# A backward pass over a KV cache: the third boundary and the opening of the last pass put into written order

## The chip, the cores and the metric

The kernel runs on one core of a Trainium2 chip. The metric is device time in microseconds, lowest wins. Three runs of the kernel before gave 1979.25 to 1979.58 us, median 1979.43. One further execution was profiled; it took 1976.74 us, and the views of the profile (the page, windows, waits, timeline) come from it.

The engines: PE is TensorE (PEld its weight loads), DVE is VectorE, ACT is ScalarE, POOL is GpSimd, SP is SyncE, which here only issues transfers. SPq, ACTq and POOLq are the queues on which these engines issue DMA.

## What is computed

Two attention layers and two MLP layers alternate (A, B, A, B, with the same weights both times), for one token; the kernel returns the output and the gradients of all weights and of the KV cache.

```python
def _A_ref(x, k_cache, v_cache, wq, wo):          # 32 heads of 128, 4 KV groups, 65536 positions
    q = (x @ wq).reshape(B, Sq, Hq, Dh).transpose(0, 2, 1, 3)
    k = jnp.repeat(k_cache, rep, axis=1)
    v = jnp.repeat(v_cache, rep, axis=1)
    p = _softmax(jnp.einsum("bhqd,bhkd->bhqk", q, k) * (Dh ** -0.5), axis=-1)
    o = jnp.einsum("bhqk,bhkd->bhqd", p, v)
    return o.transpose(0, 2, 1, 3).reshape(B, Sq, Hq * Dh) @ wo

def _B_ref(x, w1, b1, w2, b2):                    # D = 1024, F = 3584
    r = jnp.maximum(jnp.einsum("bsd,df->bsf", x, w1) + b1, 0)
    return jnp.einsum("bsf,fd->bsd", r * r, w2) + b2

x = x + _A_ref(_layernorm(x), K, V, wq, wo);  x = x + _B_ref(_layernorm(x), w1, b1, w2, b2)
x = x + _A_ref(_layernorm(x), K, V, wq, wo);  x = x + _B_ref(_layernorm(x), w1, b1, w2, b2)
out, vjp = jax.vjp(f, x, K, V, wq, wo, w1, b1, w2, b2);  grads = vjp(grad_out)
```

## The kernel before

K and V are 67 MB each and don't fit on the chip, so the kernel makes four passes over them: forward attention of the first layer, forward of the second, backward of the second (scores' gradients and the query's), and a last pass that does the first layer's backward and writes the gradients of K and V for both layers together. Between passes lie boundaries, in which the MLP and the layernorms run and few bytes of K and V are used. The third boundary is the one between pass three and the last pass.

**The boundary.** With `dn3` from pass three, a layernorm backward (`ln_bwd`) gives `dx2`. A product with the transposed W2 gives the hidden gradient `dh2` (L1418 to L1422). Then eight dot products per partition are needed, one for each of the eight 128-row blocks of W1 (3584 long) with `dh2`: the class `RowDots`. Its method `plan` (L530) takes a list of steps. "B" is a row done on DVE and ACT: DVE multiplies the row with a broadcast of `dh2`, ACT sums it, each in two halves of 1792. "A" does both in one DVE operation per half. "P" is done on PE: eight transposes of 128 columns into a PSUM buffer, a copy to SBUF, eight matmuls of one column; four such groups a row (the last of four). "T" is like "P" with the transposes made earlier and in place. The broadcast of `dh2` (`bcast_vec`) fills area 6. A second `ln_bwd` gives `dx1`, a product with eight transposed Wo blocks (`wo_turn`, `first_transposed`) gives `dOT`, and `finish` makes from it the delta of the softmax's backward.

**The last pass** (`attn_bwd4`, L1013) is a pipeline of items, each of 8 positions' columns by 128; 64 items are a group and 32 columns (four items) a block `b`. Step `i` runs `vT(i)` (transposes of V and their evacuation), `vS(i - 2)` (matmuls of V with `dOT`, four items to a PSUM buffer; the buffer begins with a matmul that writes minus delta, and when it is full DVE multiplies it with the exponentials of both layers, POOL copies these beside it, and PE transposes the result into X^T) and `k8(i - 7)`: the query's gradient (`dq`) and two PSUM buffers of K and V gradients, evacuated by ACT or DVE, whichever has less `load`. After four items the block's gradients go to HBM on POOL's queue, 1 MB for K and 1 MB for V. `bg` holds work to be done at given steps.

**What sets the order.** The framework puts the instructions in an order of its own, within their dependencies; `in_order` (L607) ties the first instruction of a piece, on each engine, to the one before it. SP issues the transfers in written order and stands at one whose buffer isn't free. Buffers of 1 MB are `area[0..13]` and the four `e1_halves` (the exponentials of the first layer, which are parked in HBM and fetched back from `e1_away` at the end of the boundary). `ring.slot()` gives the buffer used longest ago, `ring.once` gives some areas for one time first. Areas 6 to 11 are, pair by pair, the stages of the pass's outputs. The lines around which the change lies:

```python
w1s: seven rows into ring slots (four of them e1_halves), the eighth into area[5]
for st, b in ((1, 0), (1, 2), (0, 0), (1, 3), (0, 1)):       # V 0, V 2, K 0, V 3, K 1
    streams[st].fetch(ORD4[0], b)
rd = RowDots(DC, F, dh2[:], "B2_dn", area[6], lambda: transpose(w1s[0]))
steps = [("B", 5), ("T", 0), ("P", 1), ("B", 4), ("P", 2), ("A", 7), ("B", 6), ("P", 3)]
ring.once(area[6]); streams[1].fetch(ORD4[0], 1)              # V 1, when area 6 has been read
for g in ORD4: nc.sync.dma_start(out=e_tiles[1][g], in_=e1_away[g][:, :])
og1.later(vbx1, ORD4[1], bg, 16, 5, first_rows, 30, nc.sync)  # 8 Wo rows, 256 KB each, on SP
```

`later` fetches Wo rows ahead of their dot products for the next group's `dOT`; `first_rows` has seven buffers, the first seven fetches come before the pass's own.

Of the kernel before, what the change touches and what calls it, by code (L numbers as in the profile page):

```python
# [14 lines left out]
P = 128  # L15
# [3 lines left out]
def kernel(  # L19
# [24 lines left out]
    nc = tc.nc  # L44
    NOSYNC = mybir.DependencyInfo(mybir.DependencyClass.NoSync, mybir.DependencyReason.DATA)
    D = A_x.shape[-1]
# [390 lines left out]
    class RowDots:  # L437
# [92 lines left out]
        def plan(self, steps, wt):  # L530


# [39 lines left out]

        def result(self):
            if self.pieces == 1:
                return self.y[:, :, 0]
            s = vec.tile([P, self.y.shape[1]], F32, name="rd_sum", tag="rd_sum", bufs=2)
            nc.vector.tensor_tensor(out=s[:], in0=self.y[:, :, 0], in1=self.y[:, :, 1], op=ALU.add)
            return s[:, :]
# [23 lines left out]
    def blocks(ap, i, n=1):  # L602

        return ap[:, i * 1024:(i + n) * 1024].rearrange("p (a b) -> p a b", b=P)


    def in_order(fn):  # L607

        insts = nc.cur_bb.bb.instructions
        n0 = len(insts)  # L610
        before = {}
        fn()
        new = list(insts[n0:])
        want = {i.engine for i in new}
        k = n0 - 1
        while want - set(before) and k >= max(0, n0 - 4000):
            before.setdefault(insts[k].engine, insts[k])
            k -= 1
        for i in new:
            p = before.pop(i.engine, None)  # L620
            if p is not None:
                tc.add_manual_dep(i, p.name, NOSYNC, reason="in_order")

    def pipeline(n, stages, bg=None):
        maxlag = max(l for _, l in stages)
        for i in range(n + maxlag):
            for fn, lag in stages:
                if 0 <= i - lag < n:
                    fn(i - lag)
            for fn in (bg or {}).pop(i, ()):  # L630
                in_order(fn)
        assert not bg, sorted(bg)
# [175 lines left out]
    class OutGrad:  # L808
# [28 lines left out]
        def first_transposed(self, g, dx, wT):  # L837
            dxb = tmp.tile([P, DC], BF, name="dx_b")
            nc.vector.tensor_copy(out=dxb[:], in_=dx[:])
            py = ps_bg([P, R], F32)  # L840
            for k in range(R):
                for i in range(DC):
                    nc.tensor.matmul(py[:, k:k + 1], lhsT=wT[k][i], rhs=dxb[:, i:i + 1], start=(k == 0 and i == 0),
                                     stop=(k == R - 1 and i == DC - 1), skip_group_check=True)
            nc.vector.tensor_copy(out=self.dOT[:, g * R:(g + 1) * R], in_=py[:, :])
            self.finish(g)
# [166 lines left out]
    def attn_bwd4(La, Lb, oga, ogb, order, eTa, eTb, dqT, bg, group_done, streams, more_stage, tail):  # L1013
# [3 lines left out]
        KT = Turn([blocks(small, i) for i in range(3)])  # L1017
# [7 lines left out]
        state = {}  # L1025
        kstream, vstream = streams

        def g_setup(g):
# [3 lines left out]
            nc.vector.tensor_copy(out=DOB[:, g, 0, R:R2], in_=ogb.dOT[:, sl])  # L1032
            CCf = tmp.tile([P, R4], F32, name="CCf")
# [14 lines left out]
            nc.vector.tensor_copy(out=ndt4[:, :, 0:R], in_=oga.nd2[:, sl].unsqueeze(1).to_broadcast([64, UB4, R]))  # L1048
            nc.vector.tensor_copy(out=ndt4[:, :, R:R2], in_=ogb.nd2[:, sl].unsqueeze(1).to_broadcast([64, UB4, R]))
            state[("G", g)] = GG  # L1050

# [10 lines left out]
        def vS(idx):  # L1062
            g, c8 = kit[idx]
            if idx == 0:
                g_setup(g)
            vt = state.pop(("vt", idx))
            for i in range(8):
                c = c8 + i
                slot = c % UB4
                if slot == 0:  # L1070
                    state["ps_dp"] = ps_sc([P, UB4, R2])
                    nc.tensor.matmul(state["ps_dp"][:, :, :].rearrange("p c r -> p (c r)"), lhsT=sel2[:, :],
                                     rhs=state[("ndt", g)][:, :, :].rearrange("o c r -> o (c r)"), start=True, stop=False)
# [4 lines left out]
                                 rhs=DOB[:, g, 0:w, :].rearrange("p a b -> p (a b)"), start=False, stop=last)  # L1078
                if last:
                    c0 = c - slot  # L1080
# [8 lines left out]
                    nblk = UB4 // 4  # L1089
                    pt2 = ps_tr()  # L1090
                    for bi in range(nblk):
                        nc.tensor.transpose(pt2[:, bi, :], X[:, 4 * bi:4 * bi + 4, :].rearrange("p a b -> p (a b)"), ident_b[:, :])
                    xt = XT.next()
                    evac(xt[:, 0:nblk, :], pt2[:, 0:nblk, :])
                    state[(g, c0 // UB4)] = (X, xt)
# [20 lines left out]
        def k8(idx):  # L1116
            g, c8 = kit[idx]
            if idx < n - 4:
                dq(idx)
            elif idx == n - 4:  # L1120
                for k in range(4):
                    dq(idx + k)
            u = c8 // UB4
# [24 lines left out]
            if idx >= n - 8:  # L1148
# [11 lines left out]
        pipeline(n, [(vT, 0), (vS, TLEAD), (k8, TLEAD + UB4 // 8 + 1)], bg)  # L1160
# [232 lines left out]
    wo_here = [view for _, view in slabs(A_wo, ORD4[0] * GD, R, 0, D)]  # L1393
    woT1 = {}

    def wo_turn(*ks):
        for k in ks:
            transpose(wo_here[k], None, k % 2 == 0)
            woT1[k] = [part(wo_here[k], i, P) for i in range(DC)]
    w1s = []  # L1400

    def fetch_w1b(a=None):
        v = (a if a is not None else ring.slot())[:, 0:F]
        nc.sync.dma_start(out=v, in_=B_w1[len(w1s) * P:(len(w1s) + 1) * P, :])
        w1s.append(v)
    for _ in range(7):
        fetch_w1b()
    qg3.wT = wqT
    dn3 = qg3.last_transposed(ORD3[-1])
    fetch_w1b(area[5])  # L1410
    in_order(lambda: wo_turn(0, 1))
# [4 lines left out]
    in_order(lambda: wo_turn(2, 3))  # L1416
# [7 lines left out]
    ring.remove(*e1_halves)  # L1424
    ring.once(*area[7:12])
    for st, b in ((1, 0), (1, 2), (0, 0), (1, 3), (0, 1)):
        streams[st].fetch(ORD4[0], b)
    rd = RowDots(DC, F, dh2[:], "B2_dn", area[6], lambda: transpose(w1s[0]))
    steps = [("B", 5), ("T", 0), ("P", 1), ("B", 4), ("P", 2), ("A", 7), ("B", 6), ("P", 3)]
    rd.plan([(kind, kc, w1s[kc]) for kind, kc in steps], Turn([blocks(small, i) for i in (5, 6)]))  # L1430
    wo_turn(4, 5, 6, 7)
    ring.once(area[6])
    streams[1].fetch(ORD4[0], 1)
    dxn2 = ln_bwd(rd.result(), L2["n"], L2["rstd"])
    dx1 = add_cols(dx2[:], dxn2[:], "dx1")
    og1 = OutGrad(L1, "B1")
    vbx1 = part(area[13], 3, 1024)
    og1.first_transposed(ORD4[0], dx1, woT1)
    bcast_vec(vbx1, dx1[:], DC)
    for g in ORD4:  # L1440
        nc.sync.dma_start(out=e_tiles[1][g], in_=e1_away[g][:, :])
    gb2 = add_cols(gx[:], dx2[:], "gb2")
    col_to_dram(gb2, D, out_9, nc.gpsimd)
    gb1 = add_cols(dh4[:], dh2[:], "gb1", FC)
    col_to_dram(gb1, F, out_7, nc.gpsimd)
# [3 lines left out]
    load["act"] = load["dve"] = 0.0  # L1449
# [34 lines left out]
    first_rows = Turn(wo_rows.areas + [part(area[12], i, 1024) for i in range(4)])  # L1484
    og1.later(vbx1, ORD4[1], bg, 16, 5, first_rows, 30, nc.sync)
# [26 lines left out]
    def the_end():  # L1512
        PS["end"] = True
        with tc.high_priority():
# [8 lines left out]
              lambda i: [t for _, t in zip(range(after[i]), last_tasks)])  # L1523
# [34 lines left out]
```

## Time and profile before

| what | value |
|---|---|
| median of three runs | 1979.43 us (1979.25 to 1979.58) |
| the profiled execution | 1976.74 us, span 1975.0 us |
| moved by DMA | 802.37 MB, mean 406 GB/s |
| busy shares of the span | PE 80%, PEld 66%, DVE 56%, ACT 52%, POOL 10% |
| slice 25 of 40 (1185 to 1234 us) | DMA 7 tenths, 304 GB/s |
| slices 26 to 39 | DMA 9 tenths or more |

A slice is 49.4 us. Digits are tenths of busy time (9 is 90% or more). In the windows each row is a stretch: its length, then busy microseconds of PE, PEld, DVE, ACT and POOL with the number of instructions, the clock that TensorE was granted (1.00 is full), the busy share of the 16 DMA engines, and GB/s. In the timeline each row has a start, a length, engine, line, operation, output and input, and in brackets how long the engine had been idle and who ended that. A row of waits reads: who waited, for whom, microseconds in total, times, longest.

### The profile page before, as it was taken

Reading aid. Unit: us, or ns where it says so; the run is one execution under the profiler, and the core shown is the slowest. Engines: PE = TensorE matmul, PEld = TensorE weight load, DVE = VectorE, ACT = ScalarE, POOL = GpSimd, SP = SyncE. Lnnn points to the kernel's source line nnn. Section 1 sums busy time; section 2 is a strip of 40 time slices with the busy share of each in tenths; the row PEclk is TensorE's granted clock in tenths of the full one; section 3 lists DMA queues with packets and bytes.
Section 4 is the critical chain, followed back from the end, with each engine's and each line's share of the span. In section 5 each row is a group of like instructions: output and inputs, shape, how many; then the busy total and the mean of one; then the engine's idle time right before and its main releaser. Section 6 shows DMA issues by size and latency. Waiting matters only on the chain.

```text
span 1975.0 us, 65819 instructions
## 1 busy us (share of the span) xinstructions
PE 1581.9 (80%) x29938; PEld 1306.6 (66%) x29996; DVE 1101.9 (56%) x1817; ACT 1027.1 (52%) x1300; POOL 205.6 (10%) x366
## 2 busy tenths in 40 slices
PE   7887886579887767887878886877788878888787
PEld 6887776578787756777778785555455545556453
DVE  4544431146444313745554447876677778777685
ACT  3543433034433313435444436876686767777684
POOL 0000000000000000000000001222121222222221
PEclk9999998669999976999989978999998979899897
DMA  9999999999999999999999997999999999999997
GB/s 395 425 425 421 415 405 410 409 339 425 425 420 421 424 408 400 423 419 417 416 417 389 412 403 304 396 425 424 392 422 416 412 416 410 423 398 418 422 413 297
DMA packets 115073, 802.37 MB, mean 406 GB/s; under 512 B 11356, under 2 KB 11370, under 8 KB 55914
## 3 DMA queue, kind: packets, MB, share of 16 engines
q1 hardware_dynamic: 78682, 614.64, 75.4%
q0 software_dynamic: 29200, 170.94, 21.0%
q10 hardware_dynamic: 6912, 12.59, 1.7%
q8 instruction: 234, 3.83, 0.8%
q14 instruction: 45, 0.37, 0.0%
HBM read 628.18 MB, written 169.95 MB: 404 GB/s over the span
## 4 chain that ended last, share of the span: by engine, by line
PE 37%; DMA 35%; DVE 11%; ACT 10%; issue 6%; POOL 0%; SPq 0%; ACTq 0%; another core or an unknown queue 0%; POOLq 0%; DVEq 0%
DMA pair<-in_A_v_cache_dram 11%; DMA pair<-in_A_k_cache_dram 9%; DMA out_dram<-pair 8%; PE ps_tr L712 5%; PE ps_tr L962 4%; PE ps_sc L731 4%; PE ps_gg L1134 4%; ACT small L155 3%; PE ps_acc L774 3%; PE ps_tr L1057 3%; ACT pair L155 2%; PE ps_sc L983 2%; DVE pair L158 2%; PE ps_acc L1005 2%; DVE small L158 2%
## 5 line engine op out<-in xcount | busy, mean ns | idle before, releaser
L158 DVE COPY small<-ps_tr 128x1024 bf16<-128x1024 bf16 x629 | 425.8, 687 | 310.8 <-PE ps_tr L712 177.6
L155 ACT COPY small<-ps_tr 128x1024 bf16<-128x1024 bf16 x379 | 380.7, 1014 | 370.8 <-PE ps_tr L712 208.6
L155 ACT CAST pair<-ps_gg 128x1024 bf16<-128x1024 f32 (+1 forms) x281 | 270.8, 978 | 125.8 <-PE ps_gg L1134 80.1
L158 DVE CAST pair<-ps_gg 128x1024 bf16<-128x1024 f32 (+1 forms) x211 | 248.4, 1180 | 107.0 <-PE ps_gg L1134 77.6
L712 PE MATMUL ps_tr<-ident_b,pair 128*128 128x128 bf16 x3328 | 250.1, 224 | 41.4 <-DMA pair<-in_A_k_cache_dram 30.4
L1134 PE MATMUL ps_gg<-pair,small 64*128 64x512 bf16 x1024 | 200.0, 400 | 55.3 <-ACT pair L155 15.1
L712 PEld LDWEIGHTS <-pair 128*128 128x128 bf16 x3328 | 199.8, 100 | 47.0 <-DMA pair<-in_A_k_cache_dram 33.8
L774 PE MATMUL ps_acc<-eT,pair 128*128 128x64 bf16 x3840 | 169.0, 205 | 47.4 <-DMA pair<-in_A_v_cache_dram 43.1
L1057 PE MATMUL ps_tr<-ident_b,pair 128*128 128x128 bf16 x2048 | 183.7, 229 | 19.8 <-DMA pair<-in_A_v_cache_dram 13.0
L731 PE MATMUL ps_sc<-L_qpad,small 128*128 128x64 bf16 (+7 forms) x3456 | 172.5, 193 | 17.7 <-ACT small L155 11.2
L774 PEld LDWEIGHTS <-pair 128*128 128x128 bf16 x3840 | 152.6, 104 | 51.4 <-DMA pair<-in_A_v_cache_dram 46.2
L1057 PEld LDWEIGHTS <-pair 128*128 128x128 bf16 x2048 | 131.2, 102 | 71.4 <-issue 49.6
L731 PEld LDWEIGHTS <-small 128*128 128x128 bf16 x3456 | 139.4, 99 | 29.4 <-ACT small L155 17.5
L1134 PEld LDWEIGHTS <-small 64*128 64x128 bf16 x1024 | 58.8, 94 | 108.8 <-issue 80.1
L434 ACT ACTIVATE pair<-pair 128x1024 bf16<-128x1024 bf16 (+1 forms) x99 | 108.4, 1096 | 42.0 <-DVE pair L433 41.9
L962 PE MATMUL ps_tr<-ident_b,pair 128*128 128x128 bf16 x1536 | 119.7, 226 | 12.6 <-DMA pair<-in_A_v_cache_dram 5.1
L1077 PE MATMUL ps_sc<-DOB,small 128*128 128x64 bf16 (+3 forms) x2048 | 116.0, 195 | 1.2 <-ACT small L155 0.6
L962 PEld LDWEIGHTS <-pair 128*128 128x128 bf16 x1536 | 94.7, 101 | 31.5 <-issue 23.1
L1077 PEld LDWEIGHTS <-small 128*128 128x128 bf16 x2048 | 88.9, 100 | 38.6 <-issue 33.5
L983 PE MATMUL ps_sc<-B_dOpad,small 128*128 128x64 bf16 (+7 forms) x2048 | 102.2, 192 | 14.2 <-DVE small L158 6.9
L155 ACT CAST eT<-ps_gg 128x1024 bf16<-128x1024 f32 (+1 forms) x93 | 93.2, 1003 | 38.4 <-PE ps_gg L1134 12.2
L1109 PE MATMUL ps_acc<-small,pair 128*128 128x64 bf16 (+1 forms) x2048 | 109.0, 195 | 0.5
(275 smaller groups left out, 2055.0 us busy)
## 6 DMA issues: line engine op xcount, KB each, us to landing
pair<-in_A_v_cache_dram SPq DMA_DIRECT2D x74, 2048.0 KB, 19.6
pair<-in_A_k_cache_dram SPq DMA_DIRECT2D x63, 2048.0 KB, 20.0
out_dram<-pair POOLq DMA_DIRECT2D x110, 1024.0 KB, 19.4
pair<-in_A_v_cache_dram SPq DMA_DIRECT2D x80, 1024.0 KB, 10.5
pair<-in_A_k_cache_dram SPq DMA_DIRECT2D x78, 1024.0 KB, 10.9
eT<-in_A_k_cache_dram SPq DMA_DIRECT2D x21, 2048.0 KB, 20.1
eT<-in_A_v_cache_dram SPq DMA_DIRECT2D x12, 2048.0 KB, 27.3
out_dram<-eT POOLq DMA_DIRECT2D x41, 512.0 KB, 22.9
```

Source lines behind the costliest of these rows:

```text
L155: nc.scalar.copy(out=out, in_=in_)
L158: nc.vector.tensor_copy(out=out, in_=in_)
L434: nc.scalar.activation(out=view, in_=view, func=ACTF.Copy, accum_out=ycol)
L712: nc.tensor.transpose(pt[:, i, :], kb8[:, i, :], ident_b[:, :])
L731: nc.tensor.matmul(ps_s[:, slot:slot + w, :].rearrange("p a b -> p (a b)"), lhsT=kt[:, i, :], rhs=L["qpad"][:, g, 0:w, :].rearrange("p a b ...
L774: nc.tensor.matmul(ps_o[:, :, :].rearrange("p a b -> p (a b)"), lhsT=vb8[:, i, :], rhs=eT[g][:, :, c:c + 8], start=(c == 0), stop=(c == C ...
L962: nc.tensor.transpose(pt[:, i, :], vb8[:, i, :], ident_b[:, :])
L983: nc.tensor.matmul(ps_dp[:, slot:slot + w, :].rearrange("p a b -> p (a b)"), lhsT=vt[:, i, :], rhs=dOpad[:, g, 0:w, :].rearrange("p a b -> ...
L1057: nc.tensor.transpose(pt[:, i, :], vb8[:, i, :], ident_b[:, :])
L1077: nc.tensor.matmul(ps_dp[:, slot:slot + w, :].rearrange("p a b -> p (a b)"), lhsT=vt[:, i, :], rhs=DOB[:, g, 0:w, :].rearrange("p a b -> p ...
L1109: nc.tensor.matmul(ps_dq[:, 0:w, :].rearrange("p a b -> p (a b)"), lhsT=kb8[:, i, :], rhs=X[:, sl:sl + w, :].rearrange("p a b -> p (a b)") ...
L1134: nc.tensor.matmul(pg[:, t2 * 512:(t2 + 1) * 512], lhsT=xt[64 * t2:64 * t2 + 64, blk0 + half, :], rhs=GG[64 * t2:64 * t2 + 64, :, :, :].re ...
```

## The change

- W1's rows go to other buffers: rows 5, 6, 7 to areas 3, 0, 1, rows 0, 1, 2, 3 to the four `e1_halves`. Wo's two slabs keep areas 4 and 2.
- `RowDots.plan` gets a second form, `plan_pinned`, which holds every instruction in the order in which it is written (`in_order(..., True)`). New steps: B5, transposes of row 1, T0, T1, P2, B6, Wo block 2, P3, Wo block 3, B7, P4. There is no "A". Row 0's transposes come after the broadcast instead of before it; all copies of "P" are on DVE.
- Before `dh2`, two Wo blocks are transposed instead of four. Blocks 4 to 7 come after the rows.
- Transfers on SP: K block 2 is fetched as well (into area 12), the e1 tiles come before V block 1, and `ring.arrange` sets the order of the five slots.
- Three blocks of V are transposed before the pass (`v_ahead`), the first steps of the pass stand in a written list (`opening`), and the pipeline goes on from there.
- In the first PSUM buffer of the pass, minus delta is added by the last matmul instead of the first.
- The eight Wo rows for the second group come on ACT's queue, step 24 on, fetched 8 steps ahead, three buffers. The broadcast of `dx1` and two small outputs move to steps 8, 12 and 13.
- The gradients of the first two blocks go to HBM in halves.

```diff
+        def plan_pinned(self, steps, wt):
+            N, np_ = self.N, self.pieces
+            ncb, w = N // P, N // self.pieces
+            pe = [s[1] for s in steps if not callable(s) and s[0] in "PT"]
+            py = ps_acc([P, len(pe)])
+            def step(kind, kc, view):
+                if kind == "B":
+                    for p in range(np_):
+                        dot_va(view[:, p * w:(p + 1) * w], self.vbc[:, p * w:(p + 1) * w], self.y[:, kc, p:p + 1], w)
+                    return
+                for g0 in range(0, ncb, 8):
+                    gn = min(8, ncb - g0)
+                    if kind == "P":
+                        pt = ps_tr()
+                        for i in range(gn):
+                            nc.tensor.transpose(pt[:, i, :], part(view, g0 + i, P), ident_b[:, :])
+                        t = wt.next()[:, 0:gn, :]
+                        nc.vector.tensor_copy(out=t, in_=pt[:, 0:gn, :])
+                    else:
+                        t = view[:, g0 * P:(g0 + gn) * P].rearrange("p (a b) -> p a b", b=P)
+                    for i in range(gn):
+                        cb = g0 + i
+                        nc.tensor.matmul(py[:, kc:kc + 1], lhsT=t[:, i, :], rhs=self.vcb[:, cb:cb + 1], start=(kc == pe[0] and cb == 0),
+                                         stop=(kc == pe[-1] and cb == ncb - 1), skip_group_check=True)
+            for s in steps:
+                in_order(s if callable(s) else lambda: step(*s), True)
+            nc.vector.tensor_copy(out=self.y[:, 0:len(pe), 0], in_=py[:, :])
...
-    def in_order(fn):
+    def in_order(fn, each=False):
...
                 tc.add_manual_dep(i, p.name, NOSYNC, reason="in_order")
+            if each:
+                before[i.engine] = i
...
+        state = {("vt", idx): vt for idx, vt in enumerate(vts)}
...
+                first = idx < UB4 // 8
+                def minus(**flags):
+                    nc.tensor.matmul(state["ps_dp"][:, :, :].rearrange("p c r -> p (c r)"), lhsT=sel2[:, :],
+                                     rhs=state[("ndt", g)][:, :, :].rearrange("o c r -> o (c r)"), **flags)
...
+                if last:
+                    if first:
+                        minus(start=False, stop=True, skip_group_check=True)
...
-            if idx >= n - 8:
+            if idx < 8 or idx >= n - 8:
                 if j0 % 16 == 8:
                     js = slice(j0 - 8, j0 + 8)
...
+        g0 = order[0]
+        state["opening"] = True
+        g_scores(g0)
+        opening = [(g_grads, g0), (vS, 0), (vT, 3), (vS, 1), (vT, 4), (vS, 2), (vT, 5), (vS, 3), (vT, 6), (xT, g0, 0), (grads, 0), (vS, 4),
+                   (grads, 1), (vT, 7), (vS, 5), (grads, 2), (dq, 0), (dq, 1), (grads, 3), (dq, 2), (dq, 3)]
+        for fn, *args in opening:
+            in_order(lambda: fn(*args), True)
+        state["opening"] = False
+        pipeline(n, [(vT, 0), (vS, TLEAD), (k8, TLEAD + UB4 // 8 + 1)], bg, (8, 6, 4))
...
-            transpose(wo_here[k], None, k % 2 == 0)
+            transpose(wo_here[k], None, k != R - 1)
...
+    for kc, a in ((5, area[3]), (6, area[0]), (7, area[1]), (0, e1_halves[0]), (1, e1_halves[1]), (2, e1_halves[3]), (3, e1_halves[2])):
+        fetch_w1b(kc, a)
...
-    in_order(lambda: wo_turn(0, 1))
+    in_order(lambda: wo_turn(0))
...
-    in_order(lambda: wo_turn(2, 3))
+    in_order(lambda: wo_turn(1))
...
-    ring.remove(*e1_halves)
-    ring.once(*area[7:12])
-    for st, b in ((1, 0), (1, 2), (0, 0), (1, 3), (0, 1)):
+    ring.arrange(area[3], area[0], area[1], area[4], area[2])
+    ring.once(*area[7:13])
+    for st, b in ((1, 0), (1, 2), (0, 0), (1, 3), (0, 1), (0, 2)):
         streams[st].fetch(ORD4[0], b)
-    rd = RowDots(DC, F, dh2[:], "B2_dn", area[6], lambda: transpose(w1s[0]))
-    steps = [("B", 5), ("T", 0), ("P", 1), ("B", 4), ("P", 2), ("A", 7), ("B", 6), ("P", 3)]
-    rd.plan([(kind, kc, w1s[kc]) for kind, kc in steps], Turn([blocks(small, i) for i in (5, 6)]))
-    wo_turn(4, 5, 6, 7)
+    rd = RowDots(DC, F, dh2[:], "B2_dn", area[6])
+    in_order(lambda: transpose(w1b[0], None, True), True)
+    steps = [("B", 5), lambda: transpose(w1b[1], None, False), ("T", 0), ("T", 1), ("P", 2), ("B", 6), lambda: wo_turn(2), ("P", 3),
+             lambda: wo_turn(3), ("B", 7), ("P", 4)]
+    rd.plan([s if callable(s) else (*s, w1b[s[1]]) for s in steps], Turn([blocks(small, i) for i in (5, 6)]), True)
+    for g in (0, 3, 2, 1):
+        nc.sync.dma_start(out=e_tiles[1][g], in_=e1_away[g][:, :])
     ring.once(area[6])
     streams[1].fetch(ORD4[0], 1)
+    in_order(lambda: wo_turn(4, 5, 6, 7))
+    KT4, vts = Turn([blocks(small, i) for i in range(3)]), []
+    def v_ahead():
+        vb8 = streams[1].items(ORD4[0], 8 * len(vts))
+        pt = ps_tr()
+        for i in range(8):
+            nc.tensor.transpose(pt[:, i, :], vb8[:, i, :], ident_b[:, :])
+        vts.append(KT4.next())
+        nc.scalar.copy(out=vts[-1], in_=pt[:, :, :])
...
+    in_order(v_ahead)
...
-    og1.first_transposed(ORD4[0], dx1, woT1)
-    bcast_vec(vbx1, dx1[:], DC)
-    for g in ORD4:
-        nc.sync.dma_start(out=e_tiles[1][g], in_=e1_away[g][:, :])
+    og1.first_transposed(ORD4[0], dx1, woT1, v_ahead)
+    in_order(v_ahead)
...
-    load["act"] = load["dve"] = 0.0
+    load["act"], load["dve"] = 0.0, 2.5
...
-    og1.later(vbx1, ORD4[1], bg, 16, 5, first_rows, 30, nc.sync)
+    at(bg, 8, lambda: bcast_vec(vbx1, dx1[:], DC))
+    at(bg, 12, lambda: col_to_dram(gb2, D, out_9, nc.gpsimd))
+    at(bg, 13, lambda: col_to_dram(gb1, F, out_7, nc.gpsimd))
+    og1.later(vbx1, ORD4[1], bg, 24, 4, wo_rows, 8, nc.scalar)
```

## The prediction

> **What bounds the kernel now.** I read the page's 40 slices first. The DMA row stands at 9 in all slices but one and the last; that one is slice 25, 1185 to 1234 us, the third boundary. The last pass therefore ends when its bytes have been moved, plus whatever time the DMA engines stood idle. The windows (columns after the length: busy time of PE, PEld, DVE, ACT, POOL, then granted clock, DMA share, GB/s) give that idle time:
>
> ```profile
> DMA  9999999999999999999999997999999999999997
> 1184.00:1200.00 16.00, 5.56 (x100) 4.67 (x98) 13.25 (x23) 15.08 (x18) 1.24 (x2) 0.76 0.21 66
> 1200.00:1232.00 32.00, 26.52 (x425) 20.07 (x424) 20.36 (x46) 16.80 (x18) 5.76 (x10) 0.85 1.02 416
> 1232.00:1248.00 16.00, 13.46 (x219) 9.46 (x218) 13.89 (x17) 13.61 (x16) 4.20 (x8) 1.00 0.90 331
> 1248.00:1300.00 52.00, 43.94 (x686) 29.72 (x683) 40.35 (x50) 41.25 (x48) 13.58 (x23) 1.00 1.01 424
> 1300.00:1400.00 100.00, 77.68 (x1205) 53.10 (x1204) 73.69 (x124) 67.32 (x75) 25.06 (x39) 0.98 1.01 424
> ```
>
> Idle: 0.79 x 16 = 12.6 us, then 0.10 x 16 = 1.6 us, together 14.2. From 1248 on the share is full, so a microsecond of idle before that point is a microsecond at the end. The waits of SP's queue and its timeline name the two places:
>
> ```profile
> SPq L284 <- DVE pair L542: 27.9, 1, 27.9
> SPq L854 <- ACT pair L434: 21.6, 1, 21.6
> 1169.39 0.33 SPq L284 DMA_DIRECT2D pair<-in_A_k_cache_dram  x1
> 1197.71 0.33 SPq L284 DMA_DIRECT2D pair<-in_A_v_cache_dram  x1
> 1198.13 2.20 SPq L1441 DMA_DIRECT2D eT<-e_away  x4
> 1216.98 0.33 SPq L284 DMA_DIRECT2D pair<-in_A_k_cache_dram  x1
> 1239.74 0.69 SPq L284 DMA_DIRECT2D pair<-in_A_v_cache_dram  x1
> 1242.04 0.33 SPq L284 DMA_DIRECT2D pair<-in_A_k_cache_dram  x1
> ```
>
> SP stands 28 us at the fetch of V block 1 into the broadcast's area, until the last row dot (L542) has read it; four exponential tiles queue behind. The second stop looks worse than it is: the five ring slots were full by 1217, and the next read (1239.74) needs one that the compute gives back. Between 1217 and 1240 only Wo rows and outputs feed the DMA engines. So there are two limits: the row phase's end, and the step of the pass at which slots return.
>
> The compute between them, as timeline rows:
>
> ```profile
> 1197.75 0.17 DVE L577 TENSOR_TENSOR rd_sum<-B_dn 128x8 f32<-128x8 f32 x1
> 1202.15 0.17 DVE L845 COPY B_dOT<-ps_bg 128x8 f32<-128x8 f32 x1 [1.86 <-PE ps_bg L843]
> 1216.56 0.60 PE L1134 MATMUL ps_gg<-pair,small 64*128 64x512 bf16 x4
> 1225.40 0.55 POOL L1154 DMA_DIRECT2D out_dram<-pair  x1 [3.29 <-ACT pair L155]
> 1233.94 0.53 POOL L1154 DMA_DIRECT2D out_dram<-pair  x1 [3.49 <-ACT pair L155]
> ```
>
> Row sums, first dOT, first gradient, first output, second output; a block of 32 columns takes 8.5 us, while its 4.2 MB need 9.9 us of DMA at 424 GB/s. Compute that is late therefore catches up within some blocks.
>
> **What moves in the DMA work.** Before: between the end of K block 1 and the read that needs V block 4's slot (1242.04), the DMA engines moved 11 slabs of 1.05 MB (V 1, 4, 5, 6, K 2, 3, 4, two blocks' outputs), four e1 tiles and eight Wo rows of 0.26 MB. After: the same 11 slabs and tiles (K 2 now goes to area 12, V 6 takes the fifth slot), without the rows: they come on ACT's queue at steps 16 to 44, so one is there in time. The gap at 1184 is filled, since e1 tiles wait only for w1 rows 0 to 3 and the reads behind them for the three row dots. But the work then runs out earlier, and the wait at step 19 takes its place. Lost filler: 7 x 0.262 MB / 416 GB/s = 4.4 us. So the idle time becomes 14.2 + 4.4 + D, where D is how much later (or earlier) than before the compute reaches step 19. The rows cost ACT 0.33 us an issue (rows of L854 on ACT's queue, 1409 us), 2.6 us beside 20% idle; behind each stand evacuations, and each waits for transfers some eight issues back, whose data the pass has by then used, so I add 0 (bound: 8 x 1 us if one does wait). Outputs of two blocks in halves: four more POOL issues of 0.53 us, on an idle queue, and first bytes earlier, but before the point that decides: 0.
>
> **D, step by step.**
> (a) dh2: two groups of eight Wo transposes leave PE's path (the chain shows 1.74 us for each sixteen), and LN's matmul no longer waits for a DVE copy (0.9 us): -1.7 to -2.6, taken -2.0.
> (b) dh2 to row sums: 1170.71 to 1197.75 = 27.0 before, bound by ACT and DVE. After, the broadcast comes first, then T0, T1, P2, P3, P4, each instruction held: eight transposes, the copy, eight products, then the next eight transposes. PE can't run ahead of the copy, as it did before (six copies for P rows between 1179.6 and 1184.1). Columns 0.5, broadcast 7 x 0.45 = 3.3, first T0 group 1.1, four ACT copies (3 x 1.01 + 0.59) 3.6, T1's tail 2.0: 10.5. A P group at full clock: 0.65 (transposes at 1213.90, copy at 1214.55) + 0.69 + 0.06 + 0.22 = 1.62; at half clock 1.07 (1207.11 to 1208.18) + 0.69 + 0.06 + 0.25 = 2.07; the short fourth group 1.04 or 1.33. Two pairs of DVE multiplies (2.1 each) stand between the rows' copies, their transposes hidden: 2.7 or 1.9. Sum: 10.5 + 9 x 1.62 + 3 x 1.04 + 2.7 = 30.9, or 10.5 + 18.6 + 4.0 + 1.9 = 35.0. ACT's three dots (3 x 3.4 us) end earlier and hide.
>
> Which clock? These windows are pairs, each stretch with what followed:
>
> ```profile
> 649.64:653.06 3.42, 0.90 (x16) 0.91 (x17) 0.00 (x0) 0.19 (x1) 0.00 (x0) 1.00 1.03 441
> 653.06:656.47 3.41, 3.41 (x43) 3.33 (x41) 1.39 (x2) 1.83 (x2) 0.00 (x0) 0.50 0.99 413
> 1154.82:1158.23 3.41, 2.94 (x105) 2.76 (x101) 0.34 (x2) 0.00 (x0) 0.00 (x0) 1.00 1.03 410
> 1158.23:1161.65 3.42, 2.57 (x36) 2.33 (x33) 1.45 (x6) 1.01 (x1) 0.00 (x0) 0.50 1.03 420
> ```
>
> Sixteen 128-column matmuls in 3.4 us, or many narrow ones that kept PE 86% busy, and the clock fell. The P phase issues 3.41 / 1.62 x 8 = 17 transposes in such a stretch, so I take half clock after its first two groups: 35.0 - 0.9 = 34.1, D +7.1 (bounds +3.9, +8.0).
>
> The Trainium skill (TensorE: Matmul & The Clock Gate, Part 1) says the clock falls after an idle window of about 3.4 us and advises against idle gaps above that. P has none; by that rule (b) is 30.9. The 1154 row disagrees: 2.94 us busy, and the clock still fell.
>
> (c) Row sums to dx1, 2.3 before: three Wo transposes are held ahead of LN's matmul (3 x 0.87, of which 0.7 behind the statistics) and row 7's transposes and copy ahead of dx1's add on DVE (1.0): +2.9 (full clock +1.3).
> (d) dOT to first gradient: 14.4 before. After, blocks 0 to 2 are transposed beforehand; the path is two of those groups 1.7, delta and CC 0.5, four score blocks 1.7, three transposes 2.6, minus 0.4, less 1.1 as the clock opens, then DVE's pair 1.05, X's transposes 0.65, the copy 0.69: 8.2. D -6.2 (7.0 to 10.0: -7.4 to -4.4).
> (e) First gradient to step 19: vT 7 and two score blocks now come after it, with the broadcast of dx1 and two column outputs: 2.2 us of PE, less for lighter first steps: +1.0 (0 to +2.5).
> D = -2.0 + 7.1 + 2.9 - 6.2 + 1.0 = +2.8. Change: 4.4 + 2.8 = +7.2 us. The profiled execution, 1976.7 (span 1975.0), becomes 1983.9; the median of the runs is 2.7 higher, so 1986.6. Bounds: all low ends -2.6 + 3.9 + 1.3 - 7.4 = -4.8, so -0.4; all high ends -1.7 + 8.0 + 2.9 - 4.4 + 2.5 = +7.3, so +11.7.
>
> **Rivals.** 0.2% (4 us) is about what a measurement here can tell.
> 1. The clock stays open through P: -2.0 + 3.9 + 1.3 - 6.7 + 1.0 = -2.5, change +1.9, 1981.3. For it: in 618.92 to 622.34 PE was busy 1.52 us and the clock stayed; against: the pairs above. Chance 22%. (It is what the rule of the Trainium skill gives.)
> 2. Faster: PE's groups overlap DVE's copies, so that a group costs 0.75 us as at 1179.6 to 1184.1: 9 x 1.2 = 10.8 us off (b), D = -8.0, change -3.6; with the clock open as well about -6, 1973 to 1976. It decides once D is below -4.4. For it: SP's fetches are ready, and the 12.6 us are there; against: the order in which PE gets its instructions has each product ahead of the next transposes. Chance 13%.
> 3. The gap stays: if the first e1 tile waited for the last row instead of w1 rows 0 and 1, all of (b) to (e) comes on top: DMA would restart near 1207, 9 us later than at 1198, and the time is 1990 to 1993. For it: one queue, in order; against: the tiles lie only over rows 0 to 3. Chance 6%.
> Mine: 59%. Its own range 1982 to 1991. Faster by over 0.2%: rival 2 and a little: 0.14. Within: rival 1's most and the low end of mine: 0.25. Slower: 0.61. The range, 1976 to 1993, takes in rival 1, the bounds of D and half of rival 2.
>
> **What would show it.** DMA share near 1.0 from 1184 to 1212, then 0.4 to 0.7 until about 1245; row sums at 1200 to 1204; granted clock 0.50 in the P phase with PE about half busy; first gradient at 1216 to 1220; the read of K block 5 at 1243 to 1247. Row sums before 1193 or DMA full at 1225 to 1240 would prove me wrong.

## The result, and the profile after

The changed kernel takes 1985.51 us (median of 8 runs, 1981.92 to 1988.58) against 1979.34 us for the kernel before (8 runs beside them, 1976.66 to 1980.50): 1.0035 times as long, with a 95% interval of 1.0024 to 1.0045. The profiled execution took 1984.96 us, 0.5 below that median; the profiled one of before lay 2.6 below its own. So the two profiles differ by 8.2 us and the medians by 6.2.

The page's DMA row of the changed kernel, and the same windows as before (length; busy time of PE, PEld, DVE, ACT, POOL; granted clock; DMA share; GB/s):

```profile
DMA  9999999999999999999999996999999999999998
1184.00:1200.00 16.00, 10.62 (x128) 8.51 (x128) 8.63 (x13) 8.74 (x10) 0.00 (x0) 0.50 0.86 346
1200.00:1232.00 32.00, 27.12 (x440) 21.97 (x442) 19.71 (x51) 21.07 (x22) 5.64 (x10) 0.86 0.66 265
1232.00:1248.00 16.00, 14.79 (x235) 10.06 (x234) 13.16 (x17) 12.85 (x15) 6.69 (x12) 1.00 0.58 199
1248.00:1300.00 52.00, 42.63 (x673) 29.29 (x668) 40.72 (x52) 41.17 (x48) 12.21 (x22) 1.00 1.01 414
```

The gap at 1184 is nearly filled (idle 0.14 x 16 = 2.2 us, 12.6 before). In its place the DMA engines stand idle from 1212 on: 0.34 x 32 = 10.9 and 0.42 x 16 = 6.7 us. The sum is 19.8 us where it was 14.2. SP's waits between 1150 and 1260 name both places (waiter, releaser: total, times, longest):

```profile
SPq L284 <- PE ps_tr L1099: 35.9, 2, 35.2
SPq L1500 <- PE ps_tr L592: 13.7, 2, 7.8
```

L1500 is the fetch of the e1 tiles, which waits for the transposes of the P rows. L284 is the read of K block 5, which waits until `vT` (L1099) has used up V block 4. Its row and those of the compute, in the timeline:

```profile
1169.14 0.19 DVE L839 SCALAR_TENSOR_TENSOR B_dh<-ps_bg,L_r 128x28 f32<-128x28 f32 x1 [8.37 <-PE ps_bg L1486]
1202.60 0.42 DVE L609 TENSOR_TENSOR rd_sum<-B_dn 128x8 f32<-128x8 f32 x1
1208.78 0.17 DVE L881 COPY B_dOT<-ps_bg 128x8 f32<-128x8 f32 x1 [1.83 <-PE ps_bg L877]
1216.81 0.60 PE L1190 MATMUL ps_gg<-pair,small 64*128 64x512 bf16 x4 [0.79 <-DVE small L158]
1208.82 0.33 SPq L284 DMA_DIRECT2D pair<-in_A_v_cache_dram  x1
1244.48 0.33 SPq L284 DMA_DIRECT2D pair<-in_A_k_cache_dram  x1
```

From `dh2` to the row sums 33.5 us (27.0 before), from `dOT` to the first gradient 8.0 (14.4 before). SP stands from 1208.8 to 1244.5, and this is where the work has run out. Why the rows take so long is seen on PE, four rows of the timeline in the P phase:

```profile
1188.43 0.37 PE L599 MATMUL ps_acc<-rd_vcb,small 128*128 128x1 bf16 x8 [0.79 <-DVE small L594]
1188.67 1.01 PE L592 MATMUL ps_tr<-ident_b,eT 128*128 128x128 bf16 x8
1190.47 0.37 PE L599 MATMUL ps_acc<-rd_vcb,small 128*128 128x1 bf16 x8 [0.79 <-DVE small L594]
1190.70 1.01 PE L592 MATMUL ps_tr<-ident_b,eT 128*128 128x128 bf16 x8
```

Transposes, a wait of 0.79 us for DVE's copy, products, the next transposes: 2.03 us a group, at a granted clock of 0.50. PE and DVE take turns. A whole row, from one pair of DVE's multiplies to the next, takes 8.2 us:

```profile
1185.51 2.08 DVE L433 TENSOR_TENSOR pair<-pair,pair 128x1792 bf16<-128x1792 bf16 x2
1193.70 2.08 DVE L433 TENSOR_TENSOR pair<-pair,pair 128x1792 bf16<-128x1792 bf16 x2
```

### The profile page after: what moved, and what is told of

It reads as the page before. It is cut to its first block, busy times and chain, and to the rows that moved or that the text cites. A ratio compares the mean times of both kernels' runs of the same rounds, so it can differ in the third digit from the quotient of the medians.

```text
span 1983.2 us, 65950 instructions
## 1 busy us (share of the span) xinstructions
PE 1594.4 (80%) x29995; PEld 1313.7 (66%) x30052; DVE 1101.6 (56%) x1815; ACT 1032.8 (52%) x1302; POOL 205.9 (10%) x370
## 5 line engine op out<-in xcount | busy, mean ns | idle before, releaser
L155 ACT CAST pair<-ps_gg 128x1024 bf16<-128x1024 f32 (+2 forms) x286 | 277.2, 984 | 134.8 <-PE ps_gg L1190 94.7
L158 DVE CAST pair<-ps_gg 128x1024 bf16<-128x1024 f32 (+1 forms) x206 | 240.1, 1168 | 94.0 <-PE ps_gg L1190 72.3
L1099 PE MATMUL ps_tr<-ident_b,pair 128*128 128x128 bf16 x2024 | 183.7, 228 | 18.2 <-DMA pair<-in_A_v_cache_dram 13.7
L765 PE MATMUL ps_sc<-L_qpad,small 128*128 128x64 bf16 (+7 forms) x3456 | 173.2, 194 | 17.9 <-ACT small L155 10.9
L1099 PEld LDWEIGHTS <-pair 128*128 128x128 bf16 x2024 | 129.9, 102 | 75.6 <-issue 51.9
L434 ACT ACTIVATE pair<-pair 128x1024 bf16<-128x1024 bf16 (+1 forms) x105 | 118.5, 1130 | 48.3 <-DVE pair L433 48.3
L998 PEld LDWEIGHTS <-pair 128*128 128x128 bf16 x1536 | 94.3, 101 | 31.3 <-issue 21.9
L771 DVE TENSOR_REDUCE pm_all<-pair 128x8 f32<-128x512 f32 x64 | 43.9, 686 | 110.1 <-ACT pair L770 110.1
```

The lines of the kernel that those rows point to most:

```text
L155: nc.scalar.copy(out=out, in_=in_)
L158: nc.vector.tensor_copy(out=out, in_=in_)
L434: nc.scalar.activation(out=view, in_=view, func=ACTF.Copy, accum_out=ycol)
L765: nc.tensor.matmul(ps_s[:, slot:slot + w, :].rearrange("p a b -> p (a b)"), lhsT=kt[:, i, :], rhs=L["qpad"][:, g, 0:w, :].rearrange("p a b ...
L998: nc.tensor.transpose(pt[:, i, :], vb8[:, i, :], ident_b[:, :])
L1099: nc.tensor.transpose(pt[:, i, :], vb8[:, i, :], ident_b[:, :])
```

## The experiments

Each is the changed kernel with the edit shown; e7's edit stands on top of e6. For comparison across profiles, in which the boundary begins up to 3.4 us apart, times are counted from one DVE row ahead of the change, the cast of `dq_b` (1155.87 in the changed kernel, 1156.71 before). The table gives the medians, the ratio to the kernel before, the time from `dq_b` to the read of K block 5, what is left of the median when that is taken off, and the DMA idle time between 1184 and 1250 (or 1248) in the profile, from shares of windows. The experiments come from three sets of runs (e1 to e4, e5 to e8, e9 to e12), each with runs of the kernel before beside it, whose medians were 1978.8, 1978.4 and 1977.9; the ratio is taken within a set.

| kernel | median us (runs) | ratio, 95% interval | `dq_b` to K 5 | rest | idle |
|---|---|---|---|---|---|
| before | 1979.3 (8) | 1 | 85.3 | 1894.0 | 14.2 |
| changed | 1985.5 (8) | 1.0035 (1.0024 to 1.0045) | 88.6 | 1896.9 | 19.8 |
| e1_ahead | 1977.5 (11) | 0.9992 (0.9983 to 1.0001) | 79.5 | 1898.0 | 11.9 |
| e2_warm | 1982.0 (11) | 1.0018 (1.0008 to 1.0028) | 84.8 | 1897.1 | 15.8 |
| e3_rows_sp | 1980.4 (12) | 1.0010 (1.0001 to 1.0019) | 89.7 | 1890.6 | 16.0 |
| e4_whole | 1984.2 (11) | 1.0018 (1.0009 to 1.0027) | 89.0 | 1895.1 | 20.1 |
| e5_open_old | 1984.6 (7) | 1.0034 (1.0022 to 1.0046) | 91.5 | 1893.0 | 22.8 |
| e6_ahead_rows | 1972.1 (7) | 0.9965 (0.9951 to 0.9978) | 79.5 | 1892.5 | 6.6 |
| e7_ahead_rows_ln | 1975.4 (12) | 0.9980 (0.9971 to 0.9990) | 82.9 | 1892.6 | 9.4 |
| e8_tiles_last | 1984.6 (8) | 1.0027 (1.0016 to 1.0038) | 88.7 | 1895.9 | 20.1 |
| e9_open_old_again | 1985.9 (5) | 1.0039 (1.0026 to 1.0052) | 91.4 | 1894.6 | 21.9 |
| e10_after_again | 1985.4 (5) | 1.0036 (1.0023 to 1.0048) | 88.8 | 1896.6 | 19.8 |
| e11_ahead_rows_open_old | 1974.0 (12) | 0.9978 (0.9968 to 0.9988) | 82.5 | 1891.5 | 10.1 |
| e12_ahead_rows_whole | 1970.0 (5) | 0.9966 (0.9954 to 0.9979) | 79.3 | 1890.7 | 6.7 |

**e1_ahead: products one group behind.** The products of a P group are written after the next group's transposes and copy, so that PE has work while DVE copies.

```diff
+                def products(g0, gn, t):
...
+                waiting = None
                 for g0 in range(0, ncb, 8):
...
-                    for i in range(gn):
-                        nc.tensor.matmul(py[:, kc:kc + 1], lhsT=t[:, i, :], ...)
+                    if waiting is not None:
+                        products(*waiting)
+                    waiting = (g0, gn, t)
+                products(*waiting)
```

`products` holds the lines that are taken out, for the group that it is given.

> The changed kernel, with one thing different: inside a P row the eight products of a group are issued after the next group's transposes, so that PE can run ahead of DVE's copy. Theory (the held order costs time because PE and DVE take turns, 2.04 us a full group, and the end follows the compute's lateness at step 19): nine full groups fall to about 1.0 us, from dh2 to the row sums 33.5 becomes 24 to 27 us, the read of K block 5 comes 7 to 9 us earlier, and the time falls by 6 to 9 us to 1977 to 1980. Rival (the end follows the missing Wo filler alone, however late the row phase is): no change, 1985.5. Rival (DVE's own work is the bound of the row phase): less than 3 us.

Measured: 1977.5 us, 8.0 below the changed kernel. Row sums come 23.2 us after `dh2` instead of 33.5. The same stretch, PE and then DVE:

```profile
1186.88 0.35 PE L590 MATMUL ps_acc<-rd_vcb,small 128*128 128x1 bf16 x8 [0.99 <-DVE small L600]
1187.10 0.61 PE L598 MATMUL ps_tr<-ident_b,eT 128*128 128x128 bf16 x8
1187.54 0.34 PE L590 MATMUL ps_acc<-rd_vcb,small 128*128 128x1 bf16 x8
1187.75 0.38 PE L598 MATMUL ps_tr<-ident_b,eT 128*128 128x128 bf16 x4
1184.14 2.08 DVE L433 TENSOR_TENSOR pair<-pair,pair 128x1792 bf16<-128x1792 bf16 x2
1186.14 1.28 DVE L600 COPY small<-ps_tr 128x1024 bf16<-128x1024 bf16 x2
1187.74 1.02 DVE L600 COPY small<-ps_tr 128x1024 bf16<-128x1024 bf16 x2 [0.32 <-PE ps_tr L598]
1188.68 2.08 DVE L433 TENSOR_TENSOR pair<-pair,pair 128x1792 bf16<-128x1792 bf16 x2
```

Two copies run back to back, and a row with its multiplies takes 4.5 us (1184.14 to 1188.68) where it took 8.2. DVE, busy for 4.22 of these 4.54 us, is now the bound here, and the transposes run at full clock (0.61 for eight). So the order of two neighbouring lines was worth more than the whole loss.

**e2_warm: the clock alone.** Two matmuls that nobody reads, 512 and 384 columns, follow each P group's transposes; the order stays.

```diff
                         nc.vector.tensor_copy(out=t, in_=pt[:, 0:gn, :])
+                        for ncol in (512, 384):
+                            nc.tensor.matmul(ps_sc([P, 512])[:, 0:ncol], lhsT=ident_b[:, :], rhs=view[:, 0:ncol], start=True, stop=True)
```

> The changed kernel, with two matmuls whose result nobody reads (512 and 384 columns of the row, into an idle PSUM buffer) between a P group's transposes and its products, where PE waits for DVE's copy. Theory (the clock follows the columns that PE streams in about 3.4 us): the granted clock is 1.00 through the P phase, a full group takes about 1.6 us instead of 2.04, dh2 to row sums falls from 33.5 to about 30, the layernorm behind it by about 1, the time by 3 to 5 us to 1980.5 to 1982.5. Rival (the clock falls for gaps between matmuls, or for another reason that columns don't touch): clock 0.50, a group 2.1 or a little more, the time unchanged or up to 2 us longer, 1985 to 1987.

Measured: 1982.0 us. One window, first of the changed kernel and then of this one, and three PE rows of this one:

```profile
1184.00:1188.00 4.00, 2.81 (x32) 2.29 (x32) 3.00 (x5) 1.37 (x1) 0.00 (x0) 0.50 1.02 418
1184.00:1188.00 4.00, 2.80 (x46) 1.93 (x42) 3.03 (x4) 2.23 (x3) 0.00 (x0) 1.00 1.00 416
```

```profile
1187.61 0.61 PE L592 MATMUL ps_tr<-ident_b,eT 128*128 128x128 bf16 x8
1188.05 0.54 PE L596 MATMUL ps_sc<-eT,ident_b 128*128 128x512 bf16 x2
1189.22 0.61 PE L592 MATMUL ps_tr<-ident_b,eT 128*128 128x128 bf16 x8
```

The clock stays at 1.00, a group takes 1.61 us, and the row sums come 30.3 us after `dh2`. PE is busy for as long as in the changed kernel (2.80 and 2.81 of 4 us), but there eight transposes take 1.01 us instead of 0.61, so the two shares don't tell of the same work. Of the 10.3 us that e1 gains there, 3.2 are the clock's and some 7 the alternation's.

**e3_rows_sp: the filler back.** The Wo rows are fetched on SP ahead of the pass's own blocks, as before; K block 2 goes to a ring slot to make the seventh buffer free.

```diff
-    ring.once(*area[7:13])
-    for st, b in ((1, 0), (1, 2), (0, 0), (1, 3), (0, 1), (0, 2)):
+    ring.once(*area[7:12])
+    for st, b in ((1, 0), (1, 2), (0, 0), (1, 3), (0, 1)):
...
-    og1.later(vbx1, ORD4[1], bg, 24, 4, wo_rows, 8, nc.scalar)
+    first_rows = Turn(wo_rows.areas + [part(area[12], i, 1024) for i in range(4)])
+    og1.later(vbx1, ORD4[1], bg, 16, 5, first_rows, 30, nc.sync)
```

> The changed kernel, with the eight Wo rows of the second group on SP again, seven of them fetched before the pass as in the kernel before, and area 12 given to them instead of K block 2 (which goes to a ring slot). Theory (lost filler): the compute is as late as in the changed kernel, but 7 x 0.262 MB more is moved before step 19: the time falls by 3 to 4.4 us to 1981 to 1982.5. Rival (what is fetched early makes no difference, since the bytes are the same): 1985.5, within 1 us.

Measured: 1980.4 us, 5.1 below the changed kernel, although K block 5 is read 1.1 us later. The compute is no faster; the rest column falls by 6. The bytes of the rows are no longer to be moved behind that read; the prediction prices seven of them at 4.4 us. The gain lies a little above what was expected, and the scatter covers the difference (4.9 +/- 1.8 by the means against all 13 runs of the changed kernel).

**e4_whole: the first outputs whole.**

```diff
-            if idx < 8 or idx >= n - 8:
+            if idx >= n - 8:
```

> The changed kernel, with the first two blocks' gradients written whole (1 MB for K and for V) again instead of in halves. Theory (the halves only bring bytes forward to a stretch that ends before the point that decides): no change, within 1 us of 1985.5. Rival (the early first bytes are worth what they fill): 1.5 to 2.5 us longer.

Measured: 1984.2 us, 1.3 below the changed kernel by medians (2.5 +/- 1.8 by the means against all 13 runs of it), which neither expectation has. Halves bring nothing; that they cost something isn't settled by this, and in e12, with the same edit on a faster kernel, the means differ by 0.1 +/- 3.2.

**e8_tiles_last: is the gap at 1184 worth anything by itself?** The e1 tiles go behind V block 1 again, which waits for the last row dot.

```diff
-    for g in (0, 3, 2, 1):
-        nc.sync.dma_start(out=e_tiles[1][g], in_=e1_away[g][:, :])
     ring.once(area[6])
     streams[1].fetch(ORD4[0], 1)
+    for g in (0, 3, 2, 1):
+        nc.sync.dma_start(out=e_tiles[1][g], in_=e1_away[g][:, :])
```

> The four exponential tiles are fetched after V block 1 again, which waits for the last row dot; all else as changed. Theory (idle time is one sum up to step 19): the DMA engines stand idle some 8 us more between 1184 and 1198, and as much less between 1212 and 1250; the read of K block 5 stays near 1244.5 and the time at 1985.5 within 1. Rival (the gap at 1184 counts by itself): 1991 to 1994.

Measured: 1984.6 us, no longer than with the gap filled. Its windows:

```profile
1184.00:1200.00 16.00, 10.59 (x128) 8.51 (x128) 8.69 (x12) 8.74 (x10) 0.00 (x0) 0.50 0.48 191
1200.00:1232.00 32.00, 27.64 (x415) 22.58 (x415) 18.21 (x49) 19.92 (x21) 5.70 (x10) 0.77 0.89 366
1232.00:1248.00 16.00, 14.58 (x240) 10.10 (x237) 13.16 (x17) 13.23 (x14) 6.60 (x12) 1.00 0.48 166
```

Idle is now 8.3, 3.5 and 8.3 us, 20.1 together, where the changed kernel has 2.2, 10.9 and 6.7, 19.8 together. Six microseconds of idle moved from behind 1200 to ahead of it, and the time stayed. So the gap that caught the eye in the profile before isn't worth its length by itself: what is moved early is missing later, up to the same read.

**e5_open_old and e9_open_old_again: the opening undone.** The V blocks are not transposed ahead, the written list goes, minus delta is first again; e10 is the changed kernel itself, run beside the second of them.

```diff
-        opening = [(g_grads, g0), (vS, 0), (vT, 3), ...]
...
-        for fn, *args in opening:
-            in_order(lambda: fn(*args), True)
...
-        pipeline(n, [(vT, 0), (vS, TLEAD), (k8, TLEAD + UB4 // 8 + 1)], bg, (8, 6, 4))
+        pipeline(n, [(vT, 0), (vS, TLEAD), (k8, TLEAD + UB4 // 8 + 1)], bg)
...
-    in_order(v_ahead)
...
-    og1.first_transposed(ORD4[0], dx1, woT1, v_ahead)
-    in_order(v_ahead)
+    og1.first_transposed(ORD4[0], dx1, woT1)
```

> The opening alone undone: no V block is transposed ahead, and the pipeline starts from its first step as in the kernel before; all else as changed. Theory (the compute up to the read of K block 5 sets the end, one microsecond for one): dOT to first gradient goes from 8.0 back to about 14.4 us, first gradient to that read from 27.7 back to about 25.5, so the read comes about 4 us later (near 1248.7) and the time is 1989 to 1991 against 1985.5. Rival (the opening lies beside transfers that take longer anyway): 1985 to 1986.

> The opening undone, a second time, beside the changed kernel itself: the first time the read of K block 5 came 2.9 us later, as the theory had it, but the time was 1984.6, no longer than the changed kernel's. Theory (a microsecond later at that read is one at the end, and the first median was scatter): over all runs 2 to 4 us above the run of the changed kernel in this call. Rival (the lateness is made up behind the read): within 1 us of it.

> The changed kernel again, as the mark for the run before and for the scatter between calls: 1984.5 to 1986.5.

Measured: `dOT` to the first gradient is 12.5 and 12.6 us, against 8.0, and the read of K block 5 comes 2.6 to 2.9 us later than in the changed kernel. That much went as expected. The time did not: 1984.6 and 1985.9 us, by the means of 12 runs against 13 of the changed kernel 0.0 +/- 1.6. The rest column is 2 to 4 us smaller, so the lateness is made up behind the read. One place where it is can be seen in the windows, first e5_open_old, then the changed kernel:

```profile
1600.00:1700.00 100.00, 83.60 (x1079) 54.12 (x1090) 79.02 (x118) 73.54 (x92) 24.29 (x43) 0.93 1.02 422
1700.00:1800.00 100.00, 79.78 (x959) 50.09 (x967) 76.40 (x115) 74.82 (x90) 23.10 (x41) 0.97 1.00 411
```

```profile
1600.00:1700.00 100.00, 79.56 (x936) 50.44 (x941) 75.75 (x114) 70.33 (x86) 20.64 (x36) 0.88 1.01 405
1700.00:1800.00 100.00, 78.56 (x913) 49.61 (x918) 69.40 (x107) 66.46 (x81) 21.82 (x39) 0.88 0.97 372
```

Between 1600 and 1800 the old opening moves 83.3 MB, the changed kernel 77.7 (e9 and e10: 83.7 and 78.6). At 422 GB/s that is 13 us, more than there is to make up; other stretches give part of it back (from 1500 to 1600 e5_open_old moves 407 GB/s, the changed kernel 412). What makes the later stretch slow isn't known. It isn't the opening alone, since e11 has the old opening and the slow stretch (348 GB/s from 1700 to 1750). No run was made that separates it.

**e6, e11, e12: the gains together, and a better kernel.** e6 has the edits of e1 and e3; e11 adds the old opening to them, e12 the whole outputs.

> Two edits together: each P group's products after the next group's transposes (that alone gave 1977.5), and the Wo rows on SP's queue again, ahead of step 19, with K block 2 in a ring slot (that alone gave 1980.4, 5.1 us below the changed kernel). Theory (idle time of the DMA engines is one sum: time to step 19 less the bytes that can be moved before it): the gains add, 1985.5 - 8.0 - 5.1 = 1972.4, expected 1971.5 to 1974, with 7 us of idle left between 1184 and 1250. Rival (with compute earlier the rows no longer fill idle time, or push the slabs of the pass back): 1976.5 to 1978.

> The best version so far (products after the next group's transposes, Wo rows on SP's queue, 1972.05) with the opening undone as well. Theory (opening worth 3 us at the read of K block 5, and one for one at the end): 1974.5 to 1976. Rival (opening worth nothing at the end): 1971.5 to 1973.

> The best version so far with the first outputs whole again. Alone that edit gave 1984.2 against 1985.5. Theory (the halves bring bytes forward that the DMA engines take in idle time anyway, so they are worth nothing): 1971.5 to 1972.5. Rival (twice the DMAs cost the DMA engines 1 to 2 us): 1970 to 1971.

Measured: e6 1972.1, e11 1974.0, e12 1970.0 us. The two gains add (8.0 + 5.1 = 13.1; e6 is 13.4 below the changed kernel), as one sum of idle time would have it. Undoing the opening costs 1.9 by medians (2.1 +/- 2.6 by means), between the two expectations, and leaves both standing. Whole outputs give 2.0 by medians and 0.1 by means: no difference shown. The windows of e12:

```profile
1184.00:1200.00 16.00, 12.57 (x236) 11.34 (x235) 11.50 (x37) 13.27 (x16) 2.43 (x4) 0.87 1.01 413
1200.00:1232.00 32.00, 27.45 (x427) 19.59 (x424) 22.64 (x37) 23.58 (x25) 6.38 (x12) 0.96 0.79 314
1232.00:1248.00 16.00, 14.03 (x228) 10.09 (x228) 12.97 (x17) 13.64 (x17) 3.73 (x7) 1.00 1.01 374
```

6.7 us of idle are left. e6 and e12 are both faster than the kernel before, by a third of a per cent (0.9965, 0.9951 to 0.9978; 0.9966, 0.9954 to 0.9979).

**e7_ahead_rows_ln: LN's matmul first.** Three Wo transposes go behind it, all copies on ACT.

```diff
-            transpose(wo_here[k], None, k != R - 1)
+            transpose(wo_here[k], None, True)
...
-    in_order(lambda: wo_turn(4, 5, 6, 7))
+    in_order(lambda: wo_turn(4))
...
     dx1 = add_cols(dx2[:], dxn2[:], "dx1")
+    in_order(lambda: wo_turn(5, 6, 7))
```

> As the run before, and three of the four last Wo transposes behind LN's matmul instead of ahead of it, their copies all on ACT. Theory: row sums to dx_b falls from about 4.0 to about 2.5 us, and the time by 0.5 to 1.5 us more, to 1971 to 1973. Rival (the products with dx_b wait for those same transposes and copies, so that the gain is lost one step later): dx_b to dOT grows by as much, no gain, 1972.4 within 0.7.

Measured: 1975.4 us, 3.3 above e6 (3.2 +/- 2.4 by means), more than either expectation. The expected gain shrank and came back as a loss one step later, PE's rows:

```profile
1194.16 2.72 PE L625 MATMUL ps_tr<-ident_b,pair 128*128 128x128 bf16 x24
1196.67 0.34 PE L883 MATMUL ps_bg<-dx_b,pair 128*128 128x1 bf16 x6
1196.88 1.01 PE L1516 MATMUL ps_tr<-ident_b,pair 128*128 128x128 bf16 x8
1197.68 1.73 PE L883 MATMUL ps_bg<-dx_b,pair 128*128 128x1 bf16 x58
1202.62 0.59 PE L1128 MATMUL ps_sc<-DOB,small 128*128 128x64 bf16 x8 [1.05 <-ACT small L1518]
```

Row sums to `dx_b` is 3.1 us (3.3 in e6), but `dx_b` to `dOT` grows from 2.0 to 3.5, and `dOT` to the first gradient from 8.1 to 10.3. The granted clock is 0.50 from 1196 to 1204, where e6 has 0.72 and 0.86, and the last row shows PE waiting 1.05 us for ACT's copy of a transposed V block, where e6 has no such wait. So the rival's mechanism is there, and a wait for ACT and a lower clock behind it; which of the two costs how much wasn't separated.

## Why the prediction was right, point by point

The forecast of 1986.6 was 1.1 us too high. The mechanism held: the gap at 1184 filled, the idle time came back behind 1212, and the row phase in written order ran at half clock and made the read of K block 5 late. That the number is so close owes something to luck. No step of D was off by more than 1.3 us, but (a) and (e) came out 2.5 us later than put and (b), (c) and (d) 1.9 us earlier, which cancels. And one part, the opening, was worth nothing at the end, though the sum counts on it (the last point but one).

- **One sum of idle time up to the read of K block 5**: right for the boundary, and shown by e8 (the gap moved, the time stayed) and by e1, e2, e3 and e6, which take 7.9, 4.0, 3.8 and 13.2 us from the idle time and 8.0, 3.5, 5.1 and 13.4 from the medians.
- **Lost filler, 4.4**: right in kind, and its size depends on the opening. With the new opening the rest is 1895.1 to 1898.0 (mean 1896.6) where the rows come on ACT's queue (changed, e1, e2, e4, e8, e10), and 1890.6 to 1892.6 (mean 1891.6) where they come on SP's (e3, e6, e7, e12): 5.0. With the old opening it is 1893.0 and 1894.6 (e5, e9) against 1891.5 (e11): 2.3. From the kernel before to the changed one the rest grew by 2.9 only (4.9 by the two profiled executions).
- **(a) dh2, -2.0**: from `dq_b` it came only 0.7 earlier. The two Wo groups did leave, but PE's own "issue" gap in the product with W2 grew from 1.0 to 2.2 us, for which the profile shows no releaser.
- **(b) The row phase, +7.1**: +6.4. A group at half clock was put at 2.07 and took 2.03, at full clock at 1.62 and took 1.61. (The sum has a slip: 7 x 0.45 is 3.15 and not 3.3, which changes it by 0.15.)
- **(c) Row sums to `dx1`, +2.9**: +1.9, mis-sized: LN's matmul came 0.9 us late where 1.9 was put, since the three Wo transposes (2.72 us from 1202.15) began 0.45 ahead of the row sums and LN's statistics hid another 1.2; the copy of the last Wo block (number 7) ahead of `dx1`'s add cost some 0.6 for 1.0.
- **(d) The opening, -6.2**: -6.4 at the first gradient.
- **(e) First gradient to step 19, +1.0**: +2.2, mis-sized. The first gradient is earlier because work was put behind it: in e5 and e9 the first gradient moves by 4.5 us and the read by only 2.6 to 2.9.
- **D**: +3.3 where +2.8 was put.
- **"A microsecond of idle before that point is a microsecond at the end"**: right for the edits of the boundary, but not for the opening. By the prediction's own sum, (d) and (e) together, the kernel without the new opening should take 5.2 us more; the read of K block 5 came 2.6 to 2.9 us later, and the time changed by 0.0 +/- 1.6. The step had taken the pass behind 1248 as unchanged; the rest differs by 2 to 4 us between openings. So the forecast counted a gain that doesn't reach the end. What takes it back in the later part of the pass stays open.
- **Halves of the outputs, 0**: between 0 and a cost of some 2 us, not settled.

The rivals, built and measured: rival 1's kernel (the clock open) is e2, put at 1981.3, measured 1982.0. By the rule of the Trainium skill (TensorE: Matmul & The Clock Gate, Part 1), that the clock falls after an idle window of about 3.4 us, the changed kernel itself should have been that one; its PE gaps in the P phase are 0.79 us in the rows above and the clock stood at 0.50. Rival 2's (groups overlap) is e1, put at 1973 to 1976 with the clock open, measured 1977.5. Rival 3 was wrong in its price: it added the length of the gap to the time, and e8, where the tiles do wait for the last row dot, shows that the gap alone adds nothing.

## What to carry to other kernels

When the end is set by bytes, look for the last read that waits for compute: all idle time of the DMA engines ahead of it is one sum, and a visible gap earlier than that is worth filling only if the compute up to that read gets shorter or the bytes to be moved ahead of it more. When an order is held by hand, let each producer run one piece ahead of its consumer; transposes, copy and products of one group in written order make two engines take turns (8.2 us a row instead of 4.5). And price a reordering at the point that decides, here a buffer's return, not at the first result that it brings forward; then check it at the end, since the opening's gain at that return was gone there.

## What the hardware showed that was not expected

The clock followed the columns that PE streams (for each matmul, the columns of its moving operand), not PE's busy share. In these traces the granted clock changes on a grid of 3.41 us (1275 of its 1288 stretches are a multiple of that long). Here are three steps of that grid at full clock, of the changed kernel, e1_ahead and e2_warm:

```profile
1178.37:1181.78 3.41, 2.34 (x66) 1.99 (x63) 1.55 (x4) 2.15 (x4) 0.00 (x0) 1.00 1.01 423
1183.81:1187.22 3.41, 2.28 (x47) 2.05 (x48) 3.41 (x6) 1.96 (x3) 0.00 (x0) 1.00 1.00 411
1188.29:1191.70 3.41, 2.48 (x34) 1.30 (x32) 1.80 (x4) 1.84 (x3) 0.00 (x0) 1.00 0.83 345
```

PE is busy nearly as long in all three. By the matmuls that start in them it streamed 2092, 3476 and 3344 columns; the first step was followed by half clock, the others by full clock. Gaps don't tell them apart either: the longest idle time of PE is 0.79 us in the first and 0.99 in the second. Counted in the same way over all 14 profiles, there are 6649 such steps at full clock. All 420 with fewer than 2800 columns, 820 a microsecond, were followed by half clock. Of the others 6005 held full clock, the lowest with 2816 columns, and 224 lost it, so that to stay above was necessary here and not always enough; what else counts isn't known. The way back has the same border: of 630 returns to full clock none followed a step with fewer than 2784 columns. PE's busy time has none: steps that held have as little as 1.43 us of 3.41, and steps that fell as much as all of it. Some matmuls can be missing from a trace, so the border is good to a few per cent.

The DMA engines' share can stay at 1.0 while the rate falls: 405 and 422 GB/s between 1600 and 1700 in the two windows above, both with a share of 1.01 or 1.02. A share near 1 is therefore not proof that nothing is lost there.
